# Gated attention/MLP decode kernel: units 1 to 30 as a rolled loop, one `wo` load and one V transfer fewer

## The chip, the cores and the metric

The kernel runs on one core of a Trainium2 chip. The metric is device time in microseconds (us) of one execution. Before the change, three runs took 1343.45, 1343.92 and 1344.02 us; the median is 1343.92 us. A separate, profiled execution of the same kernel is what all traces below show.

## What is computed

A gate mixes an attention block over a long KV cache with a small MLP, for two batch entries of one token each:

```python
x = A_x                                                  # (2, 1, 1024), bf16
g = sigmoid((x * gate_w).sum(-1, keepdims=True))
q = (x @ wq).reshape(2, 1, 32, 128).transpose(0, 2, 1, 3)
scores = einsum("bhqd,bhkd->bhqk", q, k_cache) * 128 ** -0.5   # k_cache (2, 32, 16384, 128)
p = softmax(scores)
a = einsum("bhqk,bhkd->bhqd", p, v_cache) ... reshape(2, 1, 4096) @ wo
h = gelu(layernorm(B_x) @ w1); x1 = B_x + shift(h) @ w2  # for one token the shifted h is zero
b = x1 + gelu(layernorm(x1) @ w3) @ w4
out = g * a + (1 - g) * b                                # (2, 1, 1024)
```

Nearly all bytes are the two caches: 2 x 32 x 16384 x 128 bf16 values each, 268 MB for K and 268 MB for V, each read once.

## The kernel before

**Units.** The 32 heads are taken as 16 pairs (`HP`), and a unit is one pair of heads `hp` for one batch entry `b`, so there are 32 units: unit 2·hp+b. For each unit one transfer brings its K rows and one its V rows, 8.4 MB each, 64 KB per partition.

**Memory.** `mem` is one SBUF tensor of five cells of 32 KB per partition. K of batch entry 0 lies in cells 0 and 1, K of entry 1 in cells 1 and 2, V in cells 3 and 4 (`K_CELL`, `V_CELL`). The two K tiles share cell 1, so each K tile is scored in two halves: `score_first` reads the half that lies in cell 1, then the next K load may be issued into it, then `score_second` reads the other half.

**Scores.** `score_chunks` (L415 to L432) takes a K tile in eight chunks, four in each half: VectorE transposes a chunk into one of two `KT` buffers (L420), and TensorE runs eight matmuls on it into the PSUM tile `S` (L426). Before that GpSimd writes the query weights `qw` of the unit (`write_qw`, L357).

**Softmax and values.** `softmax_a` (L444) transposes `S` and takes maxima; `softmax_b` (L454) spreads the maximum with a TensorE matmul (L457), exponentiates on ScalarE (L464) into `pt`, and sums with a second matmul (L475). `pv` (L488) runs 64 matmuls of `pt` against V (L492). `pv_end` (L503 to L527) scales the result and folds it with 32 small matmuls (L517) into `oT`. After both units of a pair, `project` (L375) multiplies `oT` with the pair's 256 rows of `wo`, held in `wo_pair`, and adds to the PSUM row `arow` (L378).

**Order.** All large transfers are issued from SyncE's queue (SP) in program order. After a prologue (gate, MLP layers, queries, the whole of the first unit's scoring, the first V load, the first `wo` load at L603 and the first half of the second unit's scoring at L604), a Python loop writes out 15 rounds:

- `odd_rest(hp)` (L581): K load of the next pair's entry 0; second half of unit (hp, 1)'s scores; `softmax_a`; `pv` of (hp, 0); V load of (hp, 1); `pv_end(0)`; `softmax_b(1)`.
- `even_unit(hp+1)` (L590): first half of unit (hp+1, 0)'s scores; K load of (hp+1, 1); second half; `softmax_a`; `pv` of (hp, 1); V load of (hp+1, 0); `pv_end(1)`; `project` of pair hp; `wo` load of pair hp+1; `softmax_b(0)`; first half of unit (hp+1, 1)'s scores.

`last_unit` (L606) ends the kernel: V of the last unit goes into cells 0 and 1 in the pieces `PIECES` (columns of 128 values: 128, 64, 32, 16, 16), the second half of the last scores follows, `pv` and `pv_end_apart` of unit 30, the load of the last pair's `wo` rows in another layout (`wo_last`, L614) into the V cells, then `softmax_b`, `pv_last` (L534: the first two pieces as in `pv`, the rest with one small matmul per column, L548), `project`, a cast and two small output transfers. The `wo` load that `even_unit` issues for the last pair (16th) is not read by anything.

The tile framework's scheduler orders the instructions of a straight-line program on each engine by itself; the order of the calls is only its priority. A branch `LOOPED` that would roll the 15 rounds is there and switched off.

Of the kernel before, what the change touches and what calls it, by code (L numbers as in the profile page):

```python
# [23 lines left out]
def kernel(  # L24
# [15 lines left out]
    nc = tc.nc  # L40
# [10 lines left out]
    HP = H // 2  # L51
# [28 lines left out]
    def region(cell, elements, offset=0):  # L80
        at = cell * CELL + offset
        return mem[:, at : at + elements]
# [20 lines left out]
    def cache_rows(cache, hp, b):  # L103
        two = cache[b, bass.ds(2 * hp, 2)]
        return two.rearrange("h s d -> (h s) d").rearrange("(p j) d -> p (j d)", p=P)

    def load_k(hp, b):
        nc.sync.dma_start(out=region(K_CELL[b], NJ * Dh), in_=cache_rows(A_k_cache, hp, b))

    def load_v(hp, b, cell=V_CELL, pieces=(NJ,)):  # L110
        rows = cache_rows(A_v_cache, hp, b)
        j = 0
        for n in pieces:
            at = slice(j * Dh, (j + n) * Dh)
            nc.sync.dma_start(out=region(cell, NJ * Dh)[:, at], in_=rows[:, at])
            j += n
# [251 lines left out]
    def load_wo(hp):  # L368
        rows = A_wo[bass.ds(hp * 2 * Dh, 2 * Dh)]
        nc.sync.dma_start(  # L370
            out=wo_pair[:].rearrange("p t n -> p (t n)"),
            in_=rows.rearrange("(p t) n -> p (t n)", p=P),
        )

    def project(oT, weight, last):  # L375
        for t in range(2):
            for g in range(Q4):
                nc.tensor.matmul(  # L378
                    arow[QP * g : QP * g + B, :],
                    lhsT=oT[:, t, :],  # L380
                    rhs=weight[:, t, g * G1 : (g + 1) * G1],
                    start=False,
                    stop=(last and t == 1),
                    skip_group_check=True,
                )
# [51 lines left out]
    def score_first(hp, b):  # L437
        write_qw(hp, b)
        score_chunks(b, halves[1 - b], True, False)

    def score_second(b):
        score_chunks(b, halves[b], False, True)

    def softmax_a(b):  # L444
        S = S_tiles[b]
        st = ppool.tile([P, GT, QP], FP32, name="St")
        nc.vector.transpose(out=st[:].rearrange("p j r -> p (j r)"), in_=S[:])  # L447
        m = stat.tile([P, 1], FP32, name="m")
        nc.vector.tensor_reduce(out=m[:], in_=st[:, :, 0:NG], axis=AX.XY, op=ALU.max)  # L449
        Dm = ppool.tile([P, P], FP32, name="Dm")  # L450
        nc.scalar.activation(out=Dm[:], in_=ident_s[:], func=ACTF.Copy, scale=m[:, 0:1])  # L451
        st_tiles[b] = (st, Dm)

    def softmax_b(b, by_head=False):  # L454
        st, Dm = st_tiles.pop(b)
        R_ps = misc_psum([P, P])
        nc.tensor.matmul(R_ps[:], lhsT=ones_f[:], rhs=Dm[:], start=True, stop=True)  # L457
        nb = stat.tile([P, 1], FP32, name="nb")
        rs = stat.tile([P, 1], FP32, name="rs")
        parts = [slice(e * HALF, (e + 1) * HALF) for e in range(2)]  # L460
        for rows in parts:
            nc.vector.tensor_reduce(out=nb[rows], in_=R_ps[rows, rows], axis=AX.X, op=ALU.min)  # L462
        for e, rows in enumerate(parts):
            nc.scalar.activation(  # L464
                out=pts[b][rows, :, e, :].rearrange("p (m a) k -> p a k m", a=GT // 4),
                in_=st[rows, :, 0:NG].rearrange("p (a k) m -> p a k m", k=4),
                func=ACTF.Exp,
                bias=nb[rows],
                scale=scale,
                accum_out=rs[rows],  # L470
            )
        tot_ps = misc_psum([P, 2])
        rinv = rinvs[b]
        if not by_head:
            nc.tensor.matmul(tot_ps[:, 0:1], lhsT=lmat[:], rhs=rs[:], start=True, stop=True)  # L475
            nc.vector.reciprocal(out=rinv[:, 0:1], in_=tot_ps[:, 0:1])  # L476
        else:
            rs2 = stat.tile([P, 2], FP32, name="rs2")
            nc.vector.tensor_scalar(
                out=rs2[:], in0=hm2[:], scalar1=rs[:, 0:1], scalar2=None, op0=ALU.mult  # L480
            )
            nc.tensor.matmul(tot_ps[:], lhsT=ones_f[:], rhs=rs2[:], start=True, stop=True)
            nc.vector.reciprocal(out=rinv[:], in_=tot_ps[:])
            nc.vector.tensor_scalar(
                out=rinv[:], in0=rinv[:], scalar1=g_rep[:, b : b + 1], scalar2=None, op0=ALU.mult
            )

    def pv(b, g0=0, g1=NJ // 4, ng=NJ // 4, cell=V_CELL):  # L488
        V = view(cell)
        for g in range(g0, g1):  # L490
            q = g % Q4
            nc.tensor.matmul(  # L492
                oacc[b][QP * q : QP * q + 8, :],
                lhsT=pts[b][:, g].rearrange("p h k -> p (h k)"),
                rhs=V[:, 4 * g : 4 * g + 4, :].rearrange("p j d -> p (j d)"),
                start=(g < Q4),
                stop=(g >= ng - Q4),
            )
# [12 lines left out]
    def pv_end(b):  # L511
        osb = pv_rows(b, True)[:].rearrange("p (k d t) -> p k t d", k=4, t=2)
        ot = misc_psum([P, 2])
        for t in range(2):
            for k in range(4):
                for h in range(2):
                    nc.tensor.matmul(  # L517
                        ot[h * HALF : (h + 1) * HALF, t : t + 1],
                        lhsT=osb[:, k, t, :],
                        rhs=lane[:, k + 4 * h : k + 4 * h + 1],  # L520
                        start=(k == 0 and t == 0),
                        stop=(k == 3),
                        skip_group_check=True,
                    )
        nc.vector.tensor_scalar(  # L525
            out=oT[:, :, b], in0=ot[:], scalar1=g_rep[:, b : b + 1], scalar2=None, op0=ALU.mult
        )  # L527


    PIECES = (128, 64, 32, 16, 16)  # L530
    MOVED = sum(PIECES[:2])
    OTl = const.tile([P, 2, B], BF16, name="OTl")

# [20 lines left out]
    def pv_end_apart(b):  # L554
        osb = pv_rows(b, True)
        ot = misc_psum([P, 2])
        for k in range(4):
            nc.tensor.matmul(
                ot[:], lhsT=osb[:, k * Dh : (k + 1) * Dh], rhs=lane[:, k : k + 5 : 4],
                start=(k == 0), stop=(k == 3),  # L560
            )
        nc.vector.tensor_scalar(
            out=OTl[:, :, b], in0=ot[:], scalar1=g_rep[:, b : b + 1], scalar2=None, op0=ALU.mult
        )
# [14 lines left out]
    softmax_b(0)  # L579

    def odd_rest(hp):  # L581
        load_k(hp + 1, 0)
        score_second(1)
        softmax_a(1)
        pv(0)
        load_v(hp, 1)
        pv_end(0)
        softmax_b(1)

    def even_unit(hp):  # L590
        score_first(hp, 0)
        load_k(hp, 1)
        score_second(0)
        softmax_a(0)
        pv(1)
        load_v(hp, 0)
        pv_end(1)
        project(oT, wo_pair, False)
        load_wo(hp)
        softmax_b(0)  # L600
        score_first(hp, 1)

    load_wo(0)  # L603
    score_first(0, 1)  # L604

    def last_unit(hp):  # L606
        V_LAST = 0
        load_v(hp, 1, V_LAST, PIECES)
        score_second(1)
        wo_last = region(V_CELL, 2 * D).rearrange("p (h n) -> p h n", h=2)  # L610
        softmax_a(1)
        pv(0)
        pv_end_apart(0)
        nc.sync.dma_start(  # L614
            out=wo_last, in_=A_wo[(H - 2) * Dh : H * Dh].rearrange("(h d) n -> d h n", d=Dh)
        )
        softmax_b(1, by_head=True)
        pv_last(1, V_LAST)
        project(OTl, wo_last, True)
        nc.vector.tensor_copy(out=out_row[:], in_=arow[:])  # L620
        rows = out.rearrange("b s (g n) -> (b s) g n", g=Q4)
        for b, queue in enumerate((nc.sync, nc.scalar)):
            queue.dma_start(
                out=rows[b], in_=out_row[:].rearrange("(g k) n -> k g n", k=QP)[b]
            )

    LOOPED = False
    if LOOPED:
        with tc.For_i(0, HP - 1, 1, iteration_sync="reg_based") as i:
            odd_rest(i)  # L630
            even_unit(i + 1)
            with tc.If(i >= HP - 2):
                last_unit(HP - 1)
    else:
        for i in range(HP - 1):
            odd_rest(i)
            even_unit(i + 1)
        last_unit(HP - 1)


# [28 lines left out]
```

## Time and profile before

| what | before |
|---|---|
| median of three runs | 1343.92 us |
| profiled execution, its own time | 1342.64 us |
| its span (first to last instruction) | 1340.8 us |
| TensorE matmul busy | 755.4 us (56%) |
| VectorE busy | 648.7 us (48%) |
| ScalarE busy | 129.6 us (10%) |
| HBM read | 573.05 MB, 427 GB/s over the span |

The profiled execution lies 1.84 us above its own span. Two caches of 268 MB are 537 of the 573 MB; the rest is weights. In the profile's lines "L426" is line 426 of the kernel, "KT<-mem" is output and input by the program's names; a DMA line in the chain of waits runs from the issue of a transfer to its landing, and the line after it is the instruction that was waiting for it. A timeline row ends, in brackets, with how long the engine had been idle before it and who released it.

### The profile page before, as it was taken

Reading aid. Unit: us, or ns where it says so; the run is one execution under the profiler, and the core shown is the slowest. Engines: PE = TensorE matmul, PEld = TensorE weight load, DVE = VectorE, ACT = ScalarE, POOL = GpSimd, SP = SyncE. Lnnn points to the kernel's source line nnn. Section 1 sums busy time; section 2 is a strip of 40 time slices with the busy share of each in tenths; the row PEclk is TensorE's granted clock in tenths of the full one; section 3 lists DMA queues with packets and bytes.
Section 4 is the critical chain, followed back from the end, with each engine's and each line's share of the span. In section 5 each row is a group of like instructions: output and inputs, shape, how many; then the busy total and the mean of one; then the engine's idle time right before and its main releaser. Section 6 shows DMA issues by size and latency. Waiting matters only on the chain.

```text
span 1340.8 us, 12847 instructions
## 1 busy us (share of the span) xinstructions
PE 755.4 (56%) x5758; PEld 329.9 (25%) x5758; DVE 648.7 (48%) x511; ACT 129.6 (10%) x202; POOL 12.8 (1%) x47
## 2 busy tenths in 40 slices
PE   0466555566545466655546655555664555666456
PEld 0222222222222222222222222222222222222223
DVE  1255544455544445554445554444555434455543
ACT  0100011110011111001111101111100111110011
POOL 0000000000000000000000000000000000000000
PEclk9887777888777788776778877778876777887777
DMA  9999999999999999999999999999999999999997
GB/s 407 433 419 438 436 435 423 437 423 438 431 433 436 427 435 431 428 436 435 427 440 435 429 432 423 436 433 437 425 435 433 426 434 421 438 431 440 421 427 316
DMA packets 13575, 573.88 MB, mean 428 GB/s; under 512 B 1864, under 2 KB 1872, under 8 KB 4432
## 3 DMA queue, kind: packets, MB, share of 16 engines
q1 hardware_dynamic: 13096, 573.05, 99.2%
q8 instruction: 45, 0.74, 0.2%
q10 hardware_dynamic: 424, 0.01, 0.0%
q14 instruction: 10, 0.08, 0.0%
HBM read 573.05 MB, written 0.00 MB: 427 GB/s over the span
## 4 chain that ended last, share of the span: by engine, by line
DMA 72%; DVE 12%; PE 12%; issue 4%; POOL 0%; ACT 0%; ACTq 0%; DVEq 0%
DMA mem<-in_A_k_cache_dram 68%; DVE KT L420 11%; PE S L426 11%; DMA gwT<-in_gate_w_dram 2%; DMA mem<-in_A_wo_dram 1%; PE oacc L194 0%; POOL ln_rstd L265 0%; PE misc L259 0%; DVE spread L165 0%; PE misc L245 0%; DVE turn L204 0%; PE arow L378 0%; PE misc L230 0%; ACTq L85 0%; DVE out_row L620 0%
## 5 line engine op out<-in xcount | busy, mean ns | idle before, releaser
L426 PE MATMUL S<-KT,qw 128*128 128x512 bf16 x2048 | 546.3, 416 | 414.4 <-DVE KT L420 414.1
L420 DVE STREAM_TRANSPOSE KT<-mem 128x2048 f32<-128x2048 f32 x256 | 570.6, 2282 | 320.7 <-DMA mem<-in_A_k_cache_dram 270.9
L426 PEld LDWEIGHTS <-qw 128*128 128x128 bf16 x2048 | 218.5, 107 | 737.3 <-issue 557.3
L492 PE MATMUL oacc<-mem,pt 128*8 128x512 bf16 x2032 | 117.0, 383 | 0.3 <-DMA mem<-in_A_v_cache_dram 0.3
L451 ACT ACTIVATE Dm<-ident_s,m 128x128 f32<-128x128 f32 x32 | 12.9, 403 | 1026.5 <-DVE m L449 1026.5
L464 ACT ACTIVATE pt<-St,nb 64x256 bf16<-64x256 f32 x64 | 89.7, 1401 | 61.7 <-DVE nb L462 60.8
L475 PE MATMUL misc<-rs,lmat 128*128 128x1 f32 x62 | 18.2, 362 | 93.4 <-ACT pt L464 93.4
L525 DVE TENSOR_SCALAR oT<-misc,g_rep 128x2 bf16<-128x2 f32 x30 | 6.7, 222 | 129.1 <-PE misc L517 129.1
L492 PEld LDWEIGHTS <-pt 128*8 128x8 bf16 x2032 | 46.6, 87 | 67.8 <-issue 14.8
L447 DVE STREAM_TRANSPOSE St<-S 128x512 f32<-128x512 f32 x32 | 22.9, 717 | 65.8 <-PE S L426 65.8
L476 DVE RECIPROCAL rinv<-misc 128x1 f32<-128x1 f32 x31 | 5.2, 169 | 102.1 <-PE misc L475 102.1
L517 PE MATMUL misc<-lane,osb 128*64 128x1 f32 x960 | 33.8, 199 | 25.5 <-ACT osb L505 25.5
L517 PEld LDWEIGHTS misc<-lane,osb 128*64 128x64 f32 x960 | 31.3, 138 | 40.7 <-ACT osb L505 40.7
L475 PEld LDWEIGHTS misc<-rs,lmat 128*128 128x128 f32 x62 | 15.5, 311 | 101.2 <-ACT pt L464 101.2
L464 ACT ACTIVATION_READ_ACCUMULATOR pt<-St,nb 64x1 f32 x64 | 30.5, 477 | 0.0
L505 ACT ACTIVATE osb<-oacc,rinv 128x512 f32<-128x512 f32 x31 | 21.3, 687 | 58.0 <-PE oacc L492 58.0
L357 POOL TENSOR_TENSOR qw<-qdu,mask 128x16 bf16<-128x16 bf16 x32 | 8.4, 265 | 1184.7 <-PE S L426 1170.5
L462 DVE TENSOR_REDUCE nb<-misc 64x1 f32<-64x64 f32 x64 | 14.2, 222 | 9.2 <-PE misc L457 8.1
L230 PE MATMUL misc<-zp,ones_f 128*128 128x2 f32 x2 | 0.6, 363 | 31.3 <-DVE zp L228 31.3
L457 PE MATMUL misc<-Dm,ones_f 128*128 128x128 f32 x64 | 15.8, 329 | 0.0
L449 DVE TENSOR_REDUCE m<-St 128x1 f32<-128x256 f32 x32 | 13.4, 420 | 1.1
L457 PEld LDWEIGHTS misc<-Dm,ones_f 128*128 128x128 f32 x64 | 9.6, 189 | 0.7 <-issue 0.2
(95 smaller groups left out, 73.7 us busy)
## 6 DMA issues: line engine op xcount, KB each, us to landing
mem<-in_B_w_dram SPq DMA_DIRECT2D x2, 7168.0 KB, 33.0
wo_pair<-in_A_wo_dram SPq DMA_DIRECT2D x16, 512.0 KB, 32.0
mem<-in_B_w_dram SPq DMA_DIRECT2D x2, 2048.0 KB, 10.2
mem<-in_A_v_cache_dram SPq DMA_DIRECT2D x1, 4096.0 KB, 41.6
mem<-in_A_v_cache_dram SPq DMA_DIRECT2D x1, 2048.0 KB, 30.7
mem<-in_A_v_cache_dram SPq DMA_DIRECT2D x1, 1024.0 KB, 29.3
mem<-in_A_v_cache_dram SPq DMA_DIRECT2D x2, 512.0 KB, 28.4
mem<-in_A_k_cache_dram SPq DMA_DIRECT2D x32, 28.7
```

Source lines behind the costliest of these rows:

```text
L420: nc.vector.transpose(out=kt[:], in_=Kc.rearrange("p j d -> p (j d)").bitcast(FP32))
L426: nc.tensor.matmul(S, lhsT=qw[b][:, v, NG - 1 - m : NG - 1 - m + P], rhs=ktb[:, half * GT : (half + 1) * GT, w, :, e], start=(first and n ...
L447: nc.vector.transpose(out=st[:].rearrange("p j r -> p (j r)"), in_=S[:])
L449: nc.vector.tensor_reduce(out=m[:], in_=st[:, :, 0:NG], axis=AX.XY, op=ALU.max)
L451: nc.scalar.activation(out=Dm[:], in_=ident_s[:], func=ACTF.Copy, scale=m[:, 0:1])
L457: nc.tensor.matmul(R_ps[:], lhsT=ones_f[:], rhs=Dm[:], start=True, stop=True)
L462: nc.vector.tensor_reduce(out=nb[rows], in_=R_ps[rows, rows], axis=AX.X, op=ALU.min)
L464: nc.scalar.activation(out=pts[b][rows, :, e, :].rearrange("p (m a) k -> p a k m", a=GT // 4), in_=st[rows, :, 0:NG].rearrange("p (a k) m ...
L475: nc.tensor.matmul(tot_ps[:, 0:1], lhsT=lmat[:], rhs=rs[:], start=True, stop=True)
L492: nc.tensor.matmul(oacc[b][QP * q : QP * q + 8, :], lhsT=pts[b][:, g].rearrange("p h k -> p (h k)"), rhs=V[:, 4 * g : 4 * g + 4, :].rearra ...
L505: nc.scalar.activation(out=osb[:], in_=oacc[b][:], func=ACTF.Copy, scale=rinvs[b][:, 0:1] if scaled else 1.0,)
L517: nc.tensor.matmul(ot[h * HALF : (h + 1) * HALF, t : t + 1], lhsT=osb[:, k, t, :], rhs=lane[:, k + 4 * h : k + 4 * h + 1], start=(k == 0 a ...
```

## The change

The 15 rounds become a loop on the chip (`For_i`) whose body is one round, written once. Loop synchronisation "reg_based" means that semaphores are never reset and no engine waits for the others at the end of a round: a wait in the body compares a semaphore with a register that is raised in every round, and each engine branches back by itself. `in_order` ties each instruction of a block to the one written before it on the same engine, so the scheduler keeps the written order. `last_unit` becomes the arm of an `If` in the body, taken in the last round. The load of `wo_pair` moves from behind `project` in `even_unit(hp)` to the head of `odd_rest(hp)`, and the one ahead of the loop goes; so pairs 0 to 14 are loaded 15 times in all and the last pair's rows only by `wo_last`. The last V load has four pieces in place of five.

```diff
-    PIECES = (128, 64, 32, 16, 16)
+    PIECES = (128, 64, 32, 32)
...
     def odd_rest(hp):
+        load_wo(hp)
         load_k(hp + 1, 0)
         score_second(1)
...
         pv_end(1)
         project(oT, wo_pair, False)
-        load_wo(hp)
         softmax_b(0)
         score_first(hp, 1)
 
-    load_wo(0)
     score_first(0, 1)
...
-    LOOPED = False
-    if LOOPED:
-        with tc.For_i(0, HP - 1, 1, iteration_sync="reg_based") as i:
-            odd_rest(i)
-            even_unit(i + 1)
-            with tc.If(i >= HP - 2):
-                last_unit(HP - 1)
-    else:
-        for i in range(HP - 1):
-            odd_rest(i)
-            even_unit(i + 1)
-        last_unit(HP - 1)
+    def in_order():
+
+        last = {}
+        for ins in nc.cur_bb.bb.instructions:
+            if ins.engine in last:
+                tc.add_manual_dep(
+                    ins,
+                    last[ins.engine].name,
+                    mybir.DependencyInfo(
+                        mybir.DependencyClass.NoSync, mybir.DependencyReason.DATA
+                    ),
+                    reason="in order",
+                )
+            last[ins.engine] = ins
+
+    with tc.For_i(0, HP - 1, 1, iteration_sync="reg_based") as i:
+        odd_rest(i)
+        even_unit(i + 1)
+        in_order()
+        with tc.If(i >= HP - 2):
+            last_unit(HP - 1)
+            in_order()
```

## The prediction, made before the changed kernel ran

> **What bounds the kernel now.** I read the page first: the slices, the queues, the chain.
>
> ```profile
> span 1340.8 us, 12847 instructions
> PE 755.4 (56%) x5758; PEld 329.9 (25%) x5758; DVE 648.7 (48%) x511; ACT 129.6 (10%) x202; POOL 12.8 (1%) x47
> DMA  9999999999999999999999999999999999999997
> q1 hardware_dynamic: 13096, 573.05, 99.2%
> q8 instruction: 45, 0.74, 0.2%
> DMA 72%; DVE 12%; PE 12%; issue 4%; POOL 0%; ACT 0%; ACTq 0%; DVEq 0%
> ```
>
> No engine is busy more than 56% of the span, while the 16 DMA engines are at nine tenths or more in every slice but the last, and 72% of the chain is DMA. This is a streaming kernel; what changes its time is bytes, the pace of the DMA engines, or anything that leaves their queue empty. One line is small but matters here: 45 packets of instructions, 0.74 MB, travel over the same DMA engines. PE executed 5758 matmuls and 5758 weight loads, 11516 instructions, so 45 packets are one per 256 PE instructions. PE's code is streamed in while it runs.
>
> Then the pace, from the chain of waits. Each row is the first transpose after a K tile landed; two units lie between a row and the second row after it.
>
> ```profile
> 107.51 2.32 DVE KT L420
> ...
> 186.20 2.32 DVE KT L420
> ...
> 345.06 2.32 DVE KT L420
> ...
> 423.74 2.32 DVE KT L420
> ...
> 463.73 2.32 DVE KT L420
> ...
> 502.42 2.32 DVE KT L420
> ...
> 582.64 2.32 DVE KT L420
> ...
> 740.02 2.32 DVE KT L420
> ...
> 820.22 2.32 DVE KT L420
> ...
> 977.58 2.32 DVE KT L420
> ...
> 1057.82 2.32 DVE KT L420
> ...
> 1215.16 2.32 DVE KT L420
> ...
> 1295.38 2.32 DVE KT L420
> ```
>
> A regular pair of units takes 78.68 us (423.74 to 502.42): 39.99 with the `wo` load in it, 38.69 without. So `wo_pair` costs 1.30 us of DMA time and one 8.4 MB load 38.69 / 2 = 19.35 us. From 345.06 to 502.42, 582.64 to 740.02, 820.22 to 977.58 and 1057.82 to 1215.16 two pairs take 157.34 to 157.38 us, twice the regular one. But 502.42 to 582.64, 740.02 to 820.22, 977.58 to 1057.82 and 1215.16 to 1295.38 are pairs of 80.20 to 80.24 us, and the two pairs from 186.20 to 345.06 take 158.86: five excesses of 1.48 to 1.56 us, 7.6 us in all. They come 237.6 us apart. With one instruction packet per 1340.8 / 45 = 29.8 us that is once in 8 packets. My reading: the packets go round over the DMA engines, and each eighth one delays the engine that is already last, whose share every load waits for. A packet then costs 1.53 / 8 = 0.19 us of the kernel's time. The period fits; that it is the cause is inferred.
>
> Last, the slack in one unit, from the timeline.
>
> ```profile
> 409.84 0.33 SPq L115 DMA_DIRECT2D mem<-in_A_v_cache_dram  x1
> ...
> 411.70 0.49 PE L457 MATMUL misc<-Dm,ones_f 128*128 128x128 f32 x2
> ...
> 412.12 0.59 PE L378 MATMUL arow<-wo_pair,oT 128*2 128x256 bf16 x8
> ...
> 412.76 0.33 SPq L370 DMA_DIRECT2D wo_pair<-in_A_wo_dram  x1
> ...
> 423.74 4.50 DVE L420 STREAM_TRANSPOSE KT<-mem 128x2048 f32<-128x2048 f32 x2 [7.58 <-DMA mem<-in_A_k_cache_dram]
> ...
> 434.04 0.33 SPq L108 DMA_DIRECT2D mem<-in_A_k_cache_dram  x1
> ...
> 448.34 0.33 SPq L115 DMA_DIRECT2D mem<-in_A_v_cache_dram  x1
> ...
> 463.73 4.51 DVE L420 STREAM_TRANSPOSE KT<-mem 128x2048 f32<-128x2048 f32 x2 [9.07 <-DMA mem<-in_A_k_cache_dram]
> ```
>
> VectorE stands idle 7.58 or 9.07 us before each K tile lands. The K load issued at 434.04 lands at 463.73, 29.7 us later, of which 19.35 are its own: it queues for 10.3 us. The V load issued at 448.34 cannot start before 463.73 and queues for 15.4 us. Lateness on the chip below these figures never reaches the DMA engines.
>
> **The change, part by part.** Added: loop bookkeeping (raising the wait registers, addresses, the `If`, the branch back) on every engine in 15 rounds. No row shows such an instruction. Below: nothing. Above: 40 of them at the 0.17 us of the shortest VectorE operation of a round,
>
> ```profile
> L426 PE MATMUL S<-KT,qw 128*128 128x512 bf16 x2048 | 546.3, 416 | 414.4 <-DVE KT L420 414.1
> ...
> L492 PE MATMUL oacc<-mem,pt 128*8 128x512 bf16 x2032 | 117.0, 383 | 0.3 <-DMA mem<-in_A_v_cache_dram 0.3
> ...
> L475 PE MATMUL misc<-rs,lmat 128*128 128x1 f32 x62 | 18.2, 362 | 93.4 <-ACT pt L464 93.4
> ...
> L476 DVE RECIPROCAL rinv<-misc 128x1 f32<-128x1 f32 x31 | 5.2, 169 | 102.1 <-PE misc L475 102.1
> L517 PE MATMUL misc<-lane,osb 128*64 128x1 f32 x960 | 33.8, 199 | 25.5 <-ACT osb L505 25.5
> ...
> L457 PE MATMUL misc<-Dm,ones_f 128*128 128x128 f32 x64 | 15.8, 329 | 0.0
> ...
> L378 PE MATMUL arow<-wo_pair,oT 128*2 128x256 bf16 x120 | 6.3, 289 | 0.0
> ```
>
> which is 6.8 us; I take 2 us, a dozen such instructions, since a round has few waits. The boundary lies between `score_first(hp, 1)` and `score_second(1)`, that is just behind the K issue at 434.04: the last four transposes, the softmax and the V issue at 448.34 come 2 us later. Covered by the 15.4 us of V's queueing and the 9.07 us before the next tile; SP itself has nothing to issue between 412.76 and 434.04. Cost in the rounds: 0, and 0 at 6.8 us too; without that cover it would be 30 to 100 us over 15 rounds.
>
> Written order: on PE the trace has `softmax_b`'s matmul (411.70) ahead of `project` (412.12), the calls stand the other way round, so the exponentials of even units start about 1.05 us later. Inside the same cover: 0.
>
> The `wo` load at the body's head: on SP it stood behind V (409.84) and ahead of the next K (434.04), and there it stays, still waiting for `project`, with that K load behind it, 21 us away. It passes no transfer on SP, and POOL issues none. What goes is the sixteenth load: 1.30 us of queue ahead of the last V pieces.
>
> Code: a round is 2 x (64 + 64 + 32 + 2 + 2) + 8 = 336 matmuls (the counts of rows L426, L492, L517, L475, L457 over their units, and of L378 over 15 pairs), with weight loads 672 instructions, 2.6 packets. Fifteen rounds are 39 of the 45 packets. If PE keeps the loop's code (round plus arm, some 1150 instructions, 4.5 packets), then the packets end with the first round: prologue and first pass hold about 8, room for one excess, and four go: 4 x 1.53 = 6.1 us (bounds: 7.6 for all five, and a loss if packets come each round). I take 6.1, since a chip that streams one packet per 256 instructions as they come has shown no reason to fetch twice what it still holds; that is the weakest step.
>
> [...]
>
> The tail, where the chip's own chain is nearly the bound:
>
> ```profile
> 1330.67 1.04 PE L492 MATMUL oacc<-mem,pt 128*8 128x512 bf16 x16 [0.34 <-DMA mem<-in_A_v_cache_dram]
> ...
> 1335.59 0.58 PE L548 MATMUL misc<-pt,mem 128*128 128x2 bf16 x16 [0.66 <-DMA mem<-in_A_v_cache_dram]
> 1336.87 0.60 PE L378 MATMUL arow<-mem,OTl 128*2 128x256 bf16 x8 [0.70 <-DMA mem<-in_A_wo_dram]
> ```
>
> PE waited 0.34 and 0.66 us for V pieces, and `project`, ready at about 1336.43 once the last columns and their 0.2 us product were done, began only at 1336.87 with `wo_last`. With 1.30 us less ahead of the transfers these waits go: 0.34 + 0.66 + 0.44 = 1.44 us, of which the transfers themselves allow 1.30. The merged last piece puts 32 in place of 16 matmuls behind the last V landing, 0.58 us more, but PE reaches them only as the piece lands, so they are no longer than before. The arm's branch and register work lie on this chain: of 1 us, all but 1.44 - 1.30 = 0.1 shows. Bounds: 0, and 6.8 - 0.1 = 6.7 us; I take 1 us, half a round's bookkeeping, as the arm has about half a round's waits. Tail: -1.3 + 0.9 = -0.4.
>
> **Sum.** The profiled execution took 1342.64 us: 1342.64 - 6.1 - 0.4 = 1336.1. The median of the runs is 1.28 us above it, so 1337.4 us, 0.5% less. Own range: all five excesses and no delay in the arm, 1342.64 - 7.6 - 1.3 + 1.28 = 1335.0; three excesses and 2.5 us in the arm, 1342.64 - 4.6 + 1.1 + 1.28 = 1340.4.
>
> **Rivals.**
> - *Packets in every round (the other sign).* [...] It decides from 2.6 + 0.4 / (15 x 0.19) = 2.7 packets a round. For it: the trace shows packets only as code is reached, never far ahead. Against: the loop is short beside the 11516 instructions.
> - *The excesses aren't the packets'* but some other thing every 237.6 us. Then only the tail's 0.4 goes: 1343.5, no change.
> - *The boundary is longer than its cover.* PE or VectorE stands at the branch until code comes through a loaded DMA queue. From 15.4 us on (V's queueing) each further us costs 15. Small transfers at the start took 13.1 and 29.6 us to land,
>
> ```profile
> xin<-in_A_x_dram ACTq DMA_DIRECT2D x1, 4.0 KB, 13.1
> gwT<-in_gate_w_dram ACTq DMA_DIRECT2D x1, 2.0 KB, 29.6
> ```
>
> so 18 us is not out of reach: 15 x 2.6 = 39, some 1382. Against it: 45 packets came in without an idle row on PE that they would explain.
>
> **Chances and range.** Forecast 0.56, packets in every round 0.24, other cause 0.10, long boundary 0.10. About 0.2%, 2.7 us, can be told from no change; that puts the limits at 1341.2 and 1346.6. Faster 0.52 (most of the forecast's 0.56), same 0.13, slower 0.35. The range 1334.5 to 1355 holds the forecast, the other cause and most of the packets' rival, a good 0.8; the forecast's own is 1335.0 to 1340.4.
>
> **What would show it.** Right: fewer than 15 instruction packets on q8; pairs of units of 78.7 us throughout with no excess after the first rounds; VectorE still idle for 5 to 8 us before each K tile; K queueing for about 10 us. Wrong: packets at 60 or more with more excesses than before (first rival); few packets but the same excess every 237 us (second); a K or V landing preceded by less than 100% DMA share in every round (third). A last K landing (1295.38) to the cast at the end (1337.5) longer than 42 us would show the arm's branch at more than I gave it.

## The result and the profile after

The changed kernel took 1339.46 us in the median of six runs (1337.88 to 1340.40), the kernel before on the same chip 1343.66 us (six runs, 1342.97 to 1344.02): a ratio of 0.9968 [0.9956, 0.9981]. The profiled execution took 1339.33 us. The prediction, 1337.4 us, has the right sign; the result lies in its own range (1335.0 to 1340.4), 2.1 us above the forecast.

The page of the changed kernel, the same lines as before: span, engines, DMA over the slices, the two queues that matter, the chain.

```profile
span 1337.2 us, 14788 instructions
PE 771.7 (58%) x5758; PEld 336.4 (25%) x5758; DVE 651.8 (49%) x511; ACT 129.4 (10%) x202; POOL 12.8 (1%) x47
DMA  9999999999999999999999999999999999999997
q1 hardware_dynamic: 12808, 572.53, 99.2%
q8 instruction: 7, 0.11, 0.0%
DMA 4%; issue 1%; PE 1%; DVE 1%; another core or an unknown queue 1%; PEld 0%; ACT 0%; DVEq 0%; SPq 0%; PEldq 0%; ACTq 0%
```

The instructions that keep the engines busy are the same in number; the 1941 additional ones are the loop's bookkeeping (waits, register operations, branches), and the instruction packets fell from 45 to 7. The chain is no longer whole: its shares add up to a tenth of the span, because following it back breaks off in the last rounds. So the pace must be read from the timeline. Here are VectorE's transposes and SP's issues of one round, with PE's last matmuls of the body and one row of SP's list of waits (in total, times, longest, in us); a row has start, duration, engine and line, and in brackets the idle time before it and who ended that.

```profile
385.31 4.50 DVE L420 STREAM_TRANSPOSE KT<-mem 128x2048 f32<-128x2048 f32 x2 [5.47 <-DMA mem<-in_A_k_cache_dram]
...
410.30 0.33 SPq L115 DMA_DIRECT2D mem<-in_A_v_cache_dram  x1
...
424.01 4.50 DVE L420 STREAM_TRANSPOSE KT<-mem 128x2048 f32<-128x2048 f32 x2 [6.56 <-SPq L645]
...
425.07 0.33 SPq L370 DMA_DIRECT2D wo_pair<-in_A_wo_dram  x1
...
434.87 1.90 PE L426 MATMUL S<-KT,qw 128*128 128x512 bf16 x8 [0.62 <-DVEq L645]
...
437.05 8.89 DVE L420 STREAM_TRANSPOSE KT<-mem 128x2048 f32<-128x2048 f32 x4 [2.24 <-PEq L645]
437.06 0.33 SPq L108 DMA_DIRECT2D mem<-in_A_k_cache_dram  x1
...
452.11 0.33 SPq L115 DMA_DIRECT2D mem<-in_A_v_cache_dram  x1
...
464.00 2.31 DVE L420 STREAM_TRANSPOSE KT<-mem 128x2048 f32<-128x2048 f32 x1 [5.49 <-DMA mem<-in_A_k_cache_dram]
```

```profile
SPq L108 <- PEq L645: 33.3, 14, 7.0
```

A pair of units still takes 78.69 us (385.31 to 464.00), and VectorE still waits for K at its end. Inside the round the boundary shows: VectorE and PE stop for about 2 us at 437, SP issues `wo` 12 us later than before (425.07 instead of 412.76) and the K load 3 us later (437.06 instead of 434.04). K then queues for 464.00 - 437.06 - 19.35 = 7.6 us instead of 10.3. The two delays have different causes. `wo` comes late because SP, in the branch not taken (L645), waits for the K tile to land (to 424.00; more on this at `wo_back`). K comes late because at the boundary both SP's K issue and VectorE's next transpose wait for a step of PE's semaphore. PE raises it in the branch not taken, at 436.81, when its last eight matmuls of the body (434.87 + 1.90) are done; SP's wait lasts from 434.89 to 436.89 and VectorE's from 435.59 to 436.91. Before, the K issue at 434.04 followed VectorE's fourth transpose at once. So in this kernel engines do wait for one another at the end of a round, for 2.0 us in 13 of the 14 boundaries between rounds (6.9 us in the first). All of this is hidden.

To compare kernels I take the time from the landing of the second K tile to that of the last whole V tile. It holds 61 loads of 8.4 MB at 19.35 us and 15 `wo` loads at 1.27 us (20.62 - 19.35); what goes beyond these I call the **excess**. It was 7.8 us before and is 0.9 us after. The tail of the changed kernel, from the last K landing on:

```profile
1289.50 4.50 DVE L420 STREAM_TRANSPOSE KT<-mem 128x2048 f32<-128x2048 f32 x2 [5.71 <-DMA mem<-in_A_k_cache_dram]
...
1327.80 2.27 PE L548 MATMUL misc<-pt,mem 128*128 128x2 bf16 x64
1331.82 0.16 DVE L552 TENSOR_TENSOR OTl<-misc,rinv 128x2 bf16<-128x2 f32 x1 [10.47 <-remote]
1332.04 0.60 PE L378 MATMUL arow<-mem,OTl 128*2 128x256 bf16 x8 [1.96 <-DVE OTl L552]
1332.87 0.42 DVE L619 CAST out_row<-arow 128x256 bf16<-128x256 f32 x1 [0.88 <-PE arow L378]
```

and from the timeline of the kernel before:

```profile
1336.21 0.16 DVE L552 TENSOR_TENSOR OTl<-misc,rinv 128x2 bf16<-128x2 f32 x1 [8.93 <-PE misc L548]
...
1337.52 0.42 DVE L620 CAST out_row<-arow 128x256 bf16<-128x256 f32 x1 [1.15 <-PE arow L378]
```

The last K tile lands 5.88 us earlier (1295.38 before). The excess fell by more, 6.9 us; but the second K tile, from which it is counted, landed 1.0 us later in this profile (108.50) than in that of the kernel before (107.49). From the last K landing to the cast it takes 43.37 us, before 42.14: 1.23 us longer. From the cast's end to the span's end it takes 3.91 us, before 2.86: 1.05 us longer. So the span's 3.6 us are -5.88 + 1.23 + 1.05. The last columns on PE end at 1330.07, but VectorE's next instruction starts 1.75 us after them, and the profile can only call its releaser "remote". Before, that gap was 0.04 us.

The trace's own records of instructions and of semaphore steps explain this gap. In the loop's code, `$S[113]++` stands on nearly every matmul and weight load (`$S[n]++` and `$S[n]+=` raise semaphore n; times are starts, in us):

```
before   1335.958 LDWEIGHTS L548                 after    1329.854 MATMUL    L548  $S[113]++
         1335.983 MATMUL    L548                          1329.884 LDWEIGHTS L548  $S[113]++
         1335.985 LDWEIGHTS L548                          1329.914 MATMUL    L548  $S[113]++  (the last column)
         1336.010 MATMUL    L548  $S[104]+=               1329.936, .966, .996 ...  steps of semaphore 113
         1336.189 step of semaphore 104                   1331.766, 1331.796        its last two steps
         1336.212 VectorE L552                            1331.819 VectorE L552
```

Before, 385 of the 11516 matmuls and weight loads raise a semaphore; after, 8931 do. The steps come one per 30 ns. The 64 columns with their weight loads make 128 steps, 3.84 us, while PE executes them in 2.27 us. The steps fall behind, and VectorE waits for the last.

### The profile page after: what moved, and what is told of

Same layout as the page of the kernel before. It is cut to its first block, busy times and chain, and to the rows that moved or that the text cites. A ratio compares the mean times of both kernels' runs of the same rounds, so it can differ in the third digit from the quotient of the medians.

```text
span 1337.2 us, 14788 instructions
## 1 busy us (share of the span) xinstructions
PE 771.7 (58%) x5758; PEld 336.4 (25%) x5758; DVE 651.8 (49%) x511; ACT 129.4 (10%) x202; POOL 12.8 (1%) x47
## 5 line engine op out<-in xcount | busy, mean ns | idle before, releaser
L426 PE MATMUL S<-KT,qw 128*128 128x512 bf16 x2048 | 555.6, 423 | 364.1 <-DVE KT L420 358.3
L426 PEld LDWEIGHTS <-qw 128*128 128x128 bf16 x2048 | 221.6, 108 | 693.2 <-issue 520.7
L457 PE MATMUL misc<-Dm,ones_f 128*128 128x128 f32 x64 | 18.9, 384 | 0.0
```

Of the source, the lines that this page charges most:

```text
L426: nc.tensor.matmul(S, lhsT=qw[b][:, v, NG - 1 - m : NG - 1 - m + P], rhs=ktb[:, half * GT : (half + 1) * GT, w, :, e], start=(first and n ...
```

## The experiments

**Theory.** The gain is the instruction packets: some 0.19 us of the kernel's time each, gone because PE keeps the loop's code. The 2 us that are missing stand in the tail: 30 ns for each PE step, and the loop's exit. **Rivals:** the gain comes from the moved `wo` load, the four pieces or the written order, and the packets are only a companion; or the loss in the tail is the arm's branch.

### The same program written out

```diff
-    with tc.For_i(0, HP - 1, 1, iteration_sync="reg_based") as i:
+    for i in range(HP - 1):
         odd_rest(i)
         even_unit(i + 1)
-        in_order()
-        with tc.If(i >= HP - 2):
-            last_unit(HP - 1)
-            in_order()
+    last_unit(HP - 1)
```

> The changed kernel with its 15 rounds and the last unit written out by a Python loop again, without the loop on the chip and without the forced order; the four V pieces and the moved wo load stay. Theory (the gain is that PE's code is no longer streamed): 42 to 46 instruction packets again, five pairs of units of 80.2 us, the last K landing back at 1295 (1289.5 in the changed kernel), and 1342.5 us, ratio to before 0.999, since only the 1.3 us of the sixteenth wo load are gone and part of it shows. Rival (the gain comes from the wo load and the pieces): it keeps 1339.5 us, ratio 0.997. For the tail the theory says: PE's semaphore goes up in one step per group again, so the product OTl starts within 0.1 us of the last column matmul, not 1.75 us behind it.

1341.98 us (11 runs, 1341.42 to 1342.26) against 1343.34, ratio 0.9989 [0.9980, 0.9998]. The packet line of its page, and the tail from its timeline:

```profile
q8 instruction: 45, 0.74, 0.2%
```

```profile
1296.03 4.50 DVE L420 STREAM_TRANSPOSE KT<-mem 128x2048 f32<-128x2048 f32 x2 [9.08 <-DMA mem<-in_A_k_cache_dram]
...
1334.94 1.02 PE L548 MATMUL misc<-pt,mem 128*128 128x2 bf16 x32 [0.49 <-DMA mem<-in_A_v_cache_dram]
1335.99 0.16 DVE L552 TENSOR_TENSOR OTl<-misc,rinv 128x2 bf16<-128x2 f32 x1 [8.09 <-PE misc L548]
...
1336.86 0.42 DVE L619 CAST out_row<-arow 128x256 bf16<-128x256 f32 x1 [0.71 <-PE arow L378]
```

All 45 packets are back, and five excesses of 1.20 to 1.26 us with them (7.8 us in all, smaller ones included). Last K to cast is 40.83 us, 1.31 less than before: this is the one `wo` load that the prediction took off the tail, and here it arrives, because the columns' result is taken up at once (1334.94 + 1.02 = 1335.96, OTl at 1335.99). The larger last piece does cost something: 32 columns run behind the last V landing for 1.02 us, before 16 for 0.58. The 0.44 us are hidden, because before `project` stood waiting for `wo_last` that long. So the edits other than the loop are worth 1.3 us, and the loop, with its arm and its written order, the rest.

### Three rounds in the body

```diff
-    with tc.For_i(0, HP - 1, 1, iteration_sync="reg_based") as i:
-        odd_rest(i)
-        even_unit(i + 1)
+    with tc.For_i(0, HP - 1, 3, iteration_sync="reg_based") as i:
+        for r in range(3):
+            odd_rest(i + r)
+            even_unit(i + r + 1)
         in_order()
-        with tc.If(i >= HP - 2):
+        with tc.If(i >= HP - 4):
```

Beside this, `write_qw` runs on VectorE instead of GpSimd. Three rounds are 3 x 672 = 2016 matmuls and weight loads, with the arm some 2490; that this is more than PE keeps was an assumption before the run.

> The changed kernel with three rounds in the loop's body and five passes; the query weights qw are written by VectorE in place of GpSimd (about 0.1 us of VectorE per unit, in its idle time). PE's code of body and arm is then some 2250 + 500 instructions, about 11 packets. [...] Rival (what counts is the loop itself, each round's coupling or order, not the code's size): about 15 packets and 1339.5 us as in the changed kernel.

1349.43 us (4 runs, 1349.02 to 1350.30), ratio 1.0043 [1.0028, 1.0059]. The page's line:

```profile
q8 instruction: 54, 0.88, 0.3%
```

A loop that is too long for what PE keeps brings the packets back, more than the written-out program has (54 against 45), and the excess grows to 11.4 us (last K at 1299.72). This is the prediction's first rival, made real by one size. The last K tile lands 10.2 us later than in the changed kernel, the excess is 10.4 us more, and the tail is like the changed kernel's (43.81 us from K to cast), so the packets account for the difference; 11.4 us / 54 is 0.21 us each. That `write_qw` runs on another engine was not tried by itself.

### More packets in the kernel before, first form

In `softmax_b`, 128 additional small matmuls per unit; their result is read by nobody.

```diff
+            for _ in range(128):
+                nc.tensor.matmul(
+                    idle_ps[0:QP, :], lhsT=spread[:, 0, 0, :], rhs=xT[:, 0, :],
+                    start=True, stop=True, skip_group_check=True,
+                )
```

> The kernel before with 128 small matmuls more (2 columns, with their weight loads) on PE in each of 31 units, behind the sum of the softmax, where PE is idle for 10 us; their result is read by nothing. 31 x 256 instructions are 31 packets more, 76 in all. Theory (each packet costs 0.19 us of the slowest DMA engine): 31 x 0.19 = 5.9 us, 1349.5 us, ratio 1.0044, an excess of 1.5 us every 140 us in place of 237. Rival (the 237 us excess is not the packets'): time and excesses as before, 1343.7 us.

1453.26 us (5 runs), ratio 1.0819 [1.0805, 1.0834]: a miss by the experiment's design. The matmuls depend on nothing of their unit, so the scheduler ran them all at the start. The page's slices show it:

```profile
PE   0887866665555555566665555555566655555556
DMA  9323469999999999999999999999999999999997
```

PE is fullest in slices 2 to 5, DMA down at 2 to 4 tenths there, and the rounds behind them run as before (excess 7.9 us). It doesn't decide anything on the packets in the rounds.

### More packets, tied to their unit, in both kernels

The same 128 matmuls with `rhs=pts[b][:, 0, 0, 0:B]`, which each unit writes anew: once in the kernel before (31 units, 7936 more PE instructions) and once in the changed kernel.

> The kernel before with 128 small matmuls more per unit in 31 units, as in extra_before, but reading the unit's own exponentials, so that they cannot be run ahead of them; they fall into PE's idle 10 us before the next K tile. 76 packets in place of 45. Theory (packets on the slowest DMA engine, 8.1 us of excess for 45, that is 0.18 each): excess 13.7 us, 1349.0 us, ratio 1.0042. Rival (the excess has another cause): 1343.4 us, ratio 1.000, excess 8 us.

> The changed kernel with the same 128 small matmuls per unit. [...] Theory (code that stays costs no packets): 9 to 12 packets, 1339.5 us, ratio 0.997; PE's semaphore steps, 256 more of 30 ns, take 7.7 us behind each softmax and end before the next K tile lands. Rival (PE keeps only a few blocks and streams again once the body is longer than now): 100 packets or more and 1350 us or above.

In the kernel before: 1349.47 us (5 runs, 1348.48 to 1349.93) against 1343.30, ratio 1.0045 [1.0032, 1.0058]. In the changed one: 1340.30 us (12 runs, 1338.91 to 1343.81), ratio 0.9979 [0.9971, 0.9988]. From the page of the kernel before with them:

```profile
PE 871.6 (65%) x9726; PEld 446.6 (33%) x9726; DVE 648.7 (48%) x511; ACT 129.6 (10%) x202; POOL 12.8 (1%) x47
...
q8 instruction: 76, 1.25, 0.4%
```

and from the page of the changed kernel with them:

```profile
PE 958.7 (72%) x9726; PEld 522.9 (39%) x9726; DVE 652.1 (49%) x511; ACT 129.4 (10%) x202; POOL 12.8 (1%) x47
...
q8 instruction: 10, 0.16, 0.0%
```

The same work on PE costs 6.2 us where it comes as 31 more packets and about 1 us where the loop holds it (it lies 3.0 us below the kernel before, the changed kernel 3.4 and 4.2 us in its two comparisons), although PE is 72% busy there. The excess in the first is 14.0 us: (13.95 - 7.84) / 31 = 0.197 us per packet, and its steps now come about every 140 us, which is 8 x 1347.8 / 76 = 142 us. The predicted price (0.19 us, one excess per eight packets) holds for a number of packets that it wasn't made from. The rivals have no term for this difference. In the changed kernel with the additional matmuls the excess of 3.0 us lies in the first rounds, most of it before the landings at 190 and 231 us; its ten packets all start before 206 us. One step per eight packets fits the periods of both kernels; no run shows why it is eight or which DMA engine a packet met, so the prediction's reading of it stays an inference.

### One more piece folded as rows

`pv_last` takes three V pieces as `pv` does, only the last 32 columns singly: 64 PE steps in place of 128 at the end.

```diff
-    MOVED = sum(PIECES[:2])
+    MOVED = sum(PIECES[:3])
```

> The changed kernel with the first three of the last V pieces, not two, taken by the wide matmuls (the fold by 4 small matmuls stands behind the third piece), so 32 columns in place of 64 go one by one. Theory of the tail (in the loop every PE instruction raises its semaphore, one step per 30 ns, so 128 instructions run 1.75 us ahead of their own updates): 64 updates take 1.9 us against 1.1 us of PE, OTl then starts about 0.8 us behind the last column, the output 1.0 to 1.3 us earlier: 1338.3 us. Rival (the arm's branch or the transfers set the tail): no change, 1339.5 us.

> The changed kernel once more, beside the two next ones on one chip: 1339.5 us, ratio 0.9968; 7 or 8 packets, cast 43.4 us behind the last K landing.

> folded_last once more, beside the changed kernel: theory of the tail -1.3 us against it, 1338.2 us, cast 42.0 us behind the last K landing. Rival (its 1338.2 us were the spread of single runs): the same time as the changed kernel.

1338.23 us (5 runs) at first; then, beside the changed kernel on one chip, 1338.30 us (5 runs, 1336.88 to 1339.61) and the changed kernel 1339.92 us (7 runs, 1338.16 to 1340.53). The ratios to the kernel before are 0.9966 [0.9952, 0.9979] at first, then 0.9958 [0.9945, 0.9972] and for the changed kernel 0.9973 [0.9962, 0.9984]. The timeline of the second run of the folded kernel:

```profile
1290.98 4.50 DVE L420 STREAM_TRANSPOSE KT<-mem 128x2048 f32<-128x2048 f32 x2 [5.23 <-DMA mem<-in_A_k_cache_dram]
...
1329.94 0.95 PE L548 MATMUL misc<-pt,mem 128*128 128x2 bf16 x32
1332.02 0.16 DVE L552 TENSOR_TENSOR OTl<-misc,rinv 128x2 bf16<-128x2 f32 x1 [8.87 <-PE misc L548]
...
1333.06 0.42 DVE L619 CAST out_row<-arow 128x256 bf16<-128x256 f32 x1 [0.89 <-PE arow L378]
```

The gap behind the columns is 1.13 us here (64 steps are 1.92 us, executed in 0.95), and last K to cast is 42.08 us; in the changed kernel's second profile (run `changed_again`) it is 43.29. In all four profiles the tail repeats within 0.11 us: 43.37 and 43.29 changed, 41.97 and 42.08 folded. The 1.2 to 1.4 us between them are not the gap alone. It shrinks by 0.6 us (1.75 to 1.13), and the other 0.6 us come because PE has fewer columns left when they start: they end 39.9 us behind the K landing instead of 40.5 to 40.6. What the steps cost is the gap: 1.75 us behind 128 of them, 1.13 behind 64, 0.04 where the last column alone raises the semaphore. As a kernel it beats both others in the medians; its interval overlaps that of the changed kernel, so 1.6 us between the two is likely and not certain.

### All pieces folded

```diff
-    MOVED = sum(PIECES[:2])
+    MOVED = sum(PIECES)
...
-                stop=False,
+                stop=(k == 3 and MOVED == NJ),
```

> All four last V pieces go by the wide matmuls; no column matmuls are left, so the product OTl waits behind 16 PE instructions (eight of the fold and their weight loads, 0.5 us of semaphore steps) and not behind 128 (changed kernel) or 64 (folded_last). Theory: after the last V landing 0.5 us of matmuls, 0.9 of the copy, 1.0 of the fold and 0.3 of lag, 2.7 us, against 3.3 us in the changed kernel (1328.53 to 1331.82): cast 41.3 to 42.8 us behind the last K landing, 1337.7 to 1339 us. Rival (the fold on the path behind the last landing costs more than the steps saved): 44 us and 1340 us.

1339.91 us (6 runs, 1336.66 to 1340.58), ratio 0.9968 [0.9956, 0.9980]: no column steps at the end at all, and as slow as the changed kernel. Last K to cast is 43.44 us. What took the columns' place is in its timeline:

```profile
1329.16 0.60 PE L492 MATMUL oacc<-mem,pt 128*8 128x512 bf16 x8 [1.69 <-DMA mem<-in_A_v_cache_dram]
1330.70 1.87 PE L539 MATMUL misc<-lane,osb 128*128 128x2 f32 x8 [0.94 <-ACT osb L505]
1332.82 0.59 PE L378 MATMUL arow<-mem,OTl 128*2 128x256 bf16 x8 [0.25 <-DVE OTl L552]
```

PE waits 1.69 us for the last piece, and then the copy and the folding (0.94 of waiting, 1.87 of matmuls) stand behind the last landing, where single columns would have let them run ahead of it. Between the two lies the folded form.

### The last unit behind the loop

```diff
         in_order()
-        with tc.If(i >= HP - 2):
-            last_unit(HP - 1)
-            in_order()
+    last_unit(HP - 1)
```

Here the arm goes, and with it the written order of the last unit.

> The changed kernel with the last unit behind the loop, not as an arm of an If in its body. Theory: inside the loop SP no longer waits for the arm's part (the wo load is issued about 12 us earlier, the K load at the head 2.7 us earlier), which is hidden and changes nothing; at the loop's exit SP waits for the transfers in flight, the last V pieces are issued only when the V load of unit 30 has landed, 19 us after the last K tile, and the DMA queue runs empty for about 2 us: +3 us, less 1.7 us because PE's semaphore goes up once per group again: 1341 us (1339 to 1343). Rival (the arm is what costs the tail its time, the exit is free): 1337 us.

1345.46 us (10 runs, 1343.84 to 1346.31), ratio 1.0015 [1.0005, 1.0024]: a miss, slower. Its rounds are as good as the changed kernel's (8 packets, excess 0.4 us, last K at 1288.75), all the loss is behind them. The timeline at the loop's exit:

```profile
1299.28 1.90 PE L426 MATMUL S<-KT,qw 128*128 128x512 bf16 x8 [0.30 <-DVE KT L420]
1308.73 1.86 PE L492 MATMUL oacc<-mem,pt 128*8 128x512 bf16 x13 [7.55 <-PEq L671]
1308.75 2.81 SPq L115 DMA_DIRECT2D mem<-in_A_v_cache_dram  x4
1308.81 4.50 DVE L420 STREAM_TRANSPOSE KT<-mem 128x2048 f32<-128x2048 f32 x2 [9.58 <-PEq L671]
```

VectorE stands from 1299.2 and PE from 1301.2 to about 1308.7, released by a step of the loop's end (L671). The instruction records show what it waits for: at the loop's end SP waits for the V load of unit 30, which lands at 1308.07, and all engines meet behind that; the last V pieces are issued only then. With them last K to cast is 51.0 us. In the arm inside the loop the pieces are issued without this wait (at 1276.74 to 1299.84 us in the changed kernel, where V of unit 30 lands at 1308.83). PE's semaphore steps are grouped again in this tail (12 of the 472 matmuls and weight loads behind the exit raise one), which can give back no more than the 1.75 us.

### No written order

```diff
         even_unit(i + 1)
-        in_order()
         with tc.If(i >= HP - 2):
             last_unit(HP - 1)
-            in_order()
```

> The changed kernel without the forced order inside the loop: the scheduler then puts 26 of the 64 matmuls on V at the head of the body, ahead of the second half of the scores of the other unit, where PE has to wait for V to land, some 7 us. Theory (lateness under VectorE's idle time and the queueing of the loads never reaches the DMA engines): VectorE's idle time before K nearly gone in each second unit, time 1339.5 to 1341 us. Rival (written order is what makes the loop worth while): K and V issues slip past the queue, 15 x 1 to 15 x 4 us, 1355 to 1400 us.

1349.06 us (5 runs, 1345.56 to 1349.55), ratio 1.0039 [1.0026, 1.0052]; 7 packets, excess 0.8 us, last K at 1288.92. Neither theory had this: the rounds keep their pace and the arm loses. From its timeline, one round and then the arm:

```profile
442.80 1.86 PE L492 MATMUL oacc<-mem,pt 128*8 128x512 bf16 x13 [6.92 <-DMA mem<-in_A_v_cache_dram]
...
447.89 4.50 DVE L420 STREAM_TRANSPOSE KT<-mem 128x2048 f32<-128x2048 f32 x2 [7.21 <-PE S L426]
...
463.35 4.50 DVE L420 STREAM_TRANSPOSE KT<-mem 128x2048 f32<-128x2048 f32 x2
...
1313.73 4.50 DVE L420 STREAM_TRANSPOSE KT<-mem 128x2048 f32<-128x2048 f32 x2 [9.15 <-PE S L426]
```

Without the forced order, PE takes matmuls of V between two chunks of scores and waits for V there, with the scores behind it. In a round those 7 us just fit into VectorE's idle time: at 463.35 it has none left before the next K tile. In the arm no slack follows, and K to cast is 52.8 us, 9.4 more than after. The written order is worth those 9.4 us at the end and the reserve in the rounds; the fall of the packets doesn't hang on it, nor, by the run before this one, on the arm.

### The `wo` load back behind `project`

```diff
     def odd_rest(hp):
-        load_wo(hp)
         load_k(hp + 1, 0)
...
         project(oT, wo_pair, False)
+        load_wo(hp)
         softmax_b(0)
...
+    load_wo(0)
     score_first(0, 1)
```

> The changed kernel with the wo load back behind project, the first one ahead of the loop and the sixteenth, unused one again. Theory (in the loop the tail is set by PE's semaphore steps, not by the transfers): the V pieces land 1.3 us later against the last K tile, but OTl and the cast move by 0.3 us at most, 43.4 to 43.7 us behind it, 1339.5 to 1340 us. Rival (the tail still follows the transfers, as in written_out): cast 44.7 us behind, 1340.8 us.

1375.33 us (5 runs, 1373.75 to 1376.69), ratio 1.0239 [1.0225, 1.0253]: the largest miss of the study. The packets are 8, so it isn't those; the excess is 36.6 us, 2.3 to 2.8 in each round. From the timeline of this kernel, SP's issues and the landing K tiles of a round:

```profile
417.14 0.33 SPq L115 DMA_DIRECT2D mem<-in_A_v_cache_dram  x1
...
420.25 0.33 SPq L370 DMA_DIRECT2D wo_pair<-in_A_wo_dram  x1
...
430.71 4.51 DVE L420 STREAM_TRANSPOSE KT<-mem 128x2048 f32<-128x2048 f32 x2 [6.42 <-SPq L646]
...
451.35 0.33 SPq L108 DMA_DIRECT2D mem<-in_A_k_cache_dram  x1
...
473.12 4.50 DVE L420 STREAM_TRANSPOSE KT<-mem 128x2048 f32<-128x2048 f32 x2 [7.79 <-DMA mem<-in_A_k_cache_dram]
```

The K load is issued 20.6 us after the K tile that landed at 430.71 (13.05 us in the changed kernel) and lands 21.8 us after its issue, so it queued for nothing: 2.4 us beyond its own 19.35. What SP did in between, from the two kernels' lists of SP's waits (in total, times, longest):

```profile
SPq L646 <- SPq L646: 396.2, 28, 19.5
```

```profile
SPq L645 <- SPq L645: 165.7, 15, 12.5
```

SP waits on its own steps in the line of the `If`, 28 times instead of 15. The instruction records say for what (each wait here is `$S[n]>=` and `$S[n]+=` in one instruction, so it waits and then raises):

```
wo_back  420.251 issue of wo, counted on semaphore 119      after    410.301 issue of V, counted on semaphore 119
         420.635 branch of the If, not taken                         410.691 branch of the If, not taken
         421.015 waits S[115], 421.157 S[116]: at once               411.161 to .464 waits S[115], [116], [117]: at once
         430.707 wait for S[117] ends (K has landed)                 424.002 wait for S[118] ends (K has landed)
         450.064 wait for S[118] ends (V has landed)                 424.075 to .215 S[120], [121], [122]: at once
         450.135 to .281 S[120], [121], [122]: at once
         451.348 issue of K; wo's last step is at 451.302            437.062 issue of K
```

Where the arm isn't taken, SP here still has to raise every semaphore on which the arm's transfers would have counted, and waits for the transfer before on each. The arm has seven transfers (four V pieces, `wo_last`, two outputs), on 115 to 118 and 120 to 122. A round's five transfers go round over 115 to 119. So the last one that a round issues, on 119, is the only one that SP doesn't wait for. In the changed kernel this is V; with `wo` at the end of the body it is `wo`, and V comes under the wait. SP then gets to the K load when V has landed and `wo`'s 1.3 us were all that was left in the DMA queue. The queue runs dry in every round:

```profile
392.05:473.12 81.07, 45.69 (x336) 19.84 (x336) 39.74 (x28) 7.79 (x12) 0.53 (x2) 0.79 0.98 420
```

(one pair of units of this kernel: length, busy time of the engines, clock, then a DMA share of 0.98 and 420 GB/s; the changed kernel has 78.69 us, 1.00 and 433.) 15 x 2.4 = 36 us is the loss. If the transfers go on being counted in turn, an arm with five V pieces, eight transfers, would bring the same wait into the changed kernel; it wasn't tried.

What the run was made for came out too. The last V piece lands 1.27 us later behind the last K tile than in the changed kernel (40.19 us instead of 38.92), but the cast stands 43.37 us behind it in both. So it isn't the transfers that set the end in the changed kernel's tail. From its first column, 38.3 us behind K, the 128 steps at 30 ns run to 42.1 us, and the product follows at 42.3; the `wo` load that is gone buys nothing there.

## Why the prediction came out as it did

| step | predicted, us | measured, us |
|---|---|---|
| packets gone, last K landing | -6.1 | -5.88 |
| tail, last K to cast | -0.4 | +1.23 |
| cast to the span's end | 0 | +1.05 |
| profile's time over its span | 0 | +0.29 |
| profile to the median of the runs | +1.28 | +0.13 |
| **time** | **1337.4** | **1339.46** |

- **Packets.** Right in cause; the size is met in part by luck. Forty-five became seven, the pairs are 78.7 us from 424 us on, and what is left lies in the first rounds. The excess fell by 6.9 us, not 6.1; a start that was 1.0 us later in this profile hid it, and in the changed kernel's second profile, with an excess of 0.1 us, the last K tile lands 7.0 us earlier than before. The inference that the prediction called weakest, that PE keeps the loop's code, held, and the price per packet held at 76 packets. The signs named for it (fewer than 15 packets, VectorE still idle for 5 to 8 us before K) came; K queues for 7.6 us where about 10 were named.
- **What PE keeps.** Loops of some 1150 and 1650 matmuls and weight loads (the second with the additional matmuls) run on 7 and 10 packets, one of about 2490 on 54; where between 1650 and 2490 the packets come back was not measured. In the changed kernel 14 branches back over more than 1000 PE instructions brought no packet after 202 us.
- **Boundary in the rounds.** Costed at 0, and 0 it was. The cover was read right, but the reason wasn't. What shifts the round most is not a dozen bookkeeping instructions but a wait: VectorE's transposes and SP's K issue wait for PE's last matmuls of the body, SP for 2.0 us, because PE raises its semaphore in the branch not taken only behind them. With somewhat slower transposes before it (the fourth ends 10.8 us behind the landing, before 10.3) it used up 2.7 of K's 10.3 us. SP's own wait for a landing moves only `wo`.
- **`wo` at the head.** Costed at 0 because it passes no transfer on SP. In the loop that was the wrong comparison: left where it was, it would have cost 36 us. The prediction's third rival (a boundary longer than its cover) was given 0.10 and 1382 us. `wo_back` has its sign, a DMA queue that runs dry in every round (2.4 us each), and 1375.33 us, but another mechanism: SP waits for a landing, where the rival had PE or VectorE wait for code.
- **Tail: the term that failed.** "Tail: -1.3 + 0.9 = -0.4" against +2.28. The -1.3 for the transfers holds in the written-out program (1.31 us) but not in the loop, where `wo_back` has the same tail with the load put back: the steps, not the transfers, set the end. What I booked as "half a round's bookkeeping", 1 us, was mis-sized and misplaced. The front of the arm costs nothing: last K to the first matmul of L482 takes 30.79 us (to 1320.29), before 30.84. Against the written-out program the loop's tail is 2.5 us longer (43.37 to 40.83): 1.7 us is the gap of the semaphore steps, 0.7 us that PE ends the columns later behind K (its 48 matmuls on V before them take 5.16 us instead of 4.46; why stays open), the rest follows the columns' result. The prediction's sign for the arm's branch, more than 42 us from K to cast, came, but the branch isn't what it shows. The other loss is behind the cast. The records of the last 2 us show the outputs landed at 1335.2 and after them SP's waits at the loop's end (L641) and three meetings of all engines (L673) where the kernel before has two. The written-out program, without a loop, takes 3.0 us from the cast's end to the span's end, against 3.91 here and 2.86 before, so this part comes with the loop too.
- **Profile to median.** The 1.28 us that the runs lay above the profile before were one profile's luck. The changed kernel's own runs spread more (1337.88 to 1340.40): the excess in the first rounds was 0.9 in one profile and 0.1 in the other. Why the few early packets cost more in one run than in the other stays open.
- **Rivals.** Packets in every round: not in this loop (7 in all), but in one of three rounds (54 in five passes). The upper end of the prediction's range, 1355 us, rests on a number of packets a round that no run shows; three rounds in the body took 1349.43 us. Excess not the packets': refuted by the two kernels with tied matmuls. Long boundary: not here, by 7.6 us of queueing.

## What to carry to other kernels

In a kernel bound by DMA, count the instruction packets as traffic: a loop short enough for PE to keep (some 1150 and 1650 matmuls and weight loads in this case) gains about 0.2 us per packet here, and one of three times the length (54 packets) loses it all. Rolling a loop changes what ends a wait: engines can meet at the boundary (2.0 us here), and a branch not taken can make a queue wait for transfers of the arm's semaphores (2.4 us lost in each round of `wo_back`), so look at which transfer was issued last before it and whether the next large load still queues. And look at how many instructions in a short tail raise a semaphore: at 30 ns each, 128 of them took longer here than the work (3.84 us against 2.27).

## What had not been expected of the hardware

- In the loop's tail the semaphore steps of PE come one per 30 ns; a consumer of 64 small matmuls with their weight loads starts 1.75 us after the last of them has ended, of 32 1.13 us, and 0.04 us where only the last one raises the semaphore.
- 16 KB of instructions (0.74 MB / 45) cost a stream at 430 GB/s about 0.2 us of its time (excess per packet 0.17 to 0.21 us at 45, 54 and 76 packets, 0.197 for each of the 31 more), some five times what their bytes would take (16 KB / 430 GB/s = 0.04 us), and not evenly: one step of 1.0 to 1.5 us per about eight packets.
- A DMA queue that is refilled at the moment it runs dry loses 2.4 us a time here, from 21.8 us of issue to landing against 19.35.
